# Holding the preparation of a second product behind the gate, the tanh and the h of each slot, in an attention and two-product chain on one core

## The chip, the cores and the metric

The kernel runs on one core of one Trainium2 chip. The metric is the device time in microseconds (us) of one execution. Five engines matter: TensorE (PE, with its weight loads as PEld), VectorE (DVE), ScalarE (ACT), GpSimd (POOL), and SyncE (SP), which here only issues transfers. Each has a queue of its own and works through it in order.

## The reference, cut to what matters

```python
def _attn_ref(q, k, v, p):               # q, k, v: 8 x 8 heads x 576 x 64, p: 8 x 8 x 32 x 64
    ...
    p_packed = sm_attn(p, k, v)
    out = sm_attn(q, p_packed, p_packed)
    return out.astype(np.float32)

def _moe_ref(x, w_in, w_out):            # x: 4608 x 512, w_in: 512 x 2048, w_out: 2048 x 512
    h = x @ w_in
    g = h * (1.0 / (1.0 + np.exp(-h)))
    return (g @ w_out).astype(np.float32)

def _moe2_ref(x, w1, w2, w3, w_out):     # w1, w2: 512 x 1024, w3: 1024 x 1024, w_out: 1024 x 512
    a = x @ w1
    b = x @ w2
    h = a * b @ w3
    return (h @ w_out).astype(np.float32)
```

The attention's output is the x of `_moe_ref`, and its output the x of `_moe2_ref`.

## The kernel before, in words

Every matrix product is in fp32r: a matrix is split into a high part (a rounded copy, `split_hi`, line 82 on ACT or 86 on DVE) and a low part (the difference, `split_lo`, line 91, on DVE or POOL), and `mm3` (lines 98 to 100) issues three matmuls for one: high by high, low by high, high by low.

**The slots.** The attention and the first product (`_moe_ref`) run in one loop over 256 items, called slots here and counted from 0. An item is a batch b (8), a half f of its 576 columns (288) and one of 16 blocks m of the hidden dimension. `emit_h` (from line 819) issues the 6 matmuls of h into one of two PSUM banks (`ps_h`); `emit_g` (from 831) issues tanh on ACT (`sg`, line 833), the gate on DVE (`gg`, line 838, which frees the bank) and the parts of `gg` (`gh` on ACT, `gl` on POOL); `emit_x2` (from 845) issues the 12 matmuls of the second half of the product (`ps_x`) three slots later (LAG = 3). When a half is through, ACT and DVE empty the four banks of `ps_x` (`xs`). `fetch` loads the weights of h slot by slot (`mr`, on SP's queue) several slots ahead of their use; DVE makes the high part (`mq`, line 86), POOL the low one.

**What rides beside it.** In each slot the loop calls generators, paced by `due`, that issue other work: the attention of the next batches, then, from slot 209 to slot 250, `prepare_second`. This prepares the weights of the second product. The weights of `_moe2_ref` arrive as 64-bit words (`raw`, loaded by SP at line 956) and are decoded: two ACT instructions (`ps_dec` and `raw`), two on DVE (`z`, line 176, and `raw`, line 178), one on POOL (`z`, line 182). Some were decoded earlier and come from DRAM (`z` from `late_d`). The generator has these pieces:

- `step()` takes one matrix. A block of `wo2` (8 of them, the first 8 steps) is split into `o`; a block of w3 is kept; two blocks of w1 or w2 together start `combine`, which puts 11 small steps on a list: sums and differences on DVE (`sums`, line 933), and parts `w12s` (high on ACT, low on DVE) that ACT's queue stores to DRAM.
- `some(2)` runs two entries of that list.
- `turn(n)` splits a block of w3 (`w3T`: high on ACT, low on DVE).
- `product(n)` multiplies a block of w3 by four blocks of `wo2` on PE (12 matmuls of 512 columns into `ps_w`); after every second one the sum is split (`w34s`) and stored by SP.

First come 11 calls with one `step()` each, then 18 rounds of two calls: a round has one product (from the third on), one turn (up to the 16th), and in each of its two calls a step, when one is due, and `some(2)`.

**What sets the order.** The instructions are not issued in the order of the program. A scheduler orders each engine's queue at build time by a simulation of its own, keeping dependencies; an instruction that is ready early by that simulation may be put far ahead of its place in the program. `tc.issue_after(x)` binds the instructions inside the block, on the engine of x alone, to places behind x in that queue. It adds an order, no semaphore. The dictionary `behind` holds the latest such x; before the change it has the latest tanh as `behind["sg"]` and the latest gate as `behind["gg"]`, and `fetch` and the decoding of earlier slots use them already.

After the loop follow the second product's own items, with PE busy nearly throughout.

Of the kernel before, what the change touches and what calls it, by code (L numbers as in the profile page):

```python
# [23 lines left out]
def attention_swiglu_chain(  # L24
# [35 lines left out]
    KM2 = DF2 // 128  # L60
# [18 lines left out]
    V, A, T, G, DMA = nc.vector, nc.scalar, nc.tensor, nc.gpsimd, nc.sync  # L79
# [4 lines left out]
    def split_hi(hi, src, on_vector=False):  # L84
        if on_vector:
            V.tensor_copy(out=hi, in_=src)  # L86
        else:
            act_copy(hi, src)

    def split_lo(lo, src, hi, eng=None):  # L90
        (eng or V).tensor_tensor(out=lo, in0=src, in1=hi.bitcast(F32), op=ALU.subtract)  # L91

    def split(hi, lo, src, on_vector=False, eng=None):
        split_hi(hi, src, on_vector)
        split_lo(lo, src, hi, eng)

    def mm3(dst, wh, wl, xh, xl, start, stop):
        T.matmul(out=dst, lhsT=wh, rhs=xh, start=start, stop=False)  # L98
        T.matmul(out=dst, lhsT=wl, rhs=xh, start=False, stop=False)  # L99
        T.matmul(out=dst, lhsT=wh, rhs=xl, start=False, stop=stop)  # L100

    behind = {}

    def move(out, in_, eng=DMA):

        out, in_ = (x.bitcast(F32) if x.dtype == F32R else x for x in (out, in_))
        with tc.issue_after(behind[eng]) if eng in behind else ExitStack():
            return eng.dma_start(out=out, in_=in_)  # L108
# [3 lines left out]
    def store(out, in_, age=1):  # L112

        stores.append([age, out, in_])

    def flush():
        for x in list(stores):
            if x[0] <= 0:
                move(x[1], x[2], A)
                stores.remove(x)  # L120
            else:
                x[0] -= 1
# [33 lines left out]
    def bank(name):  # L156
        return ps_f.tile([128, 512], F32, tag="f", name=name)
# [94 lines left out]
    class Lane:  # L252
# [31 lines left out]
        def mm(self, dst, w, x, start, stop):  # L284

            if self.plain:
                T.matmul(out=dst, lhsT=w[0], rhs=x[0], start=start, stop=stop)
            else:
                mm3(dst, *w, *x, start, stop)
# [300 lines left out]
    def chain(units):  # L590

        seen = set()

        def once(i, what):
            if i < len(units) and (i, what) not in seen:
                seen.add((i, what))
                getattr(units[i], what)()

        i = 0
        while i < len(units):  # L600
            u = units[i]
            for what in ("load", "prepare", "turn0", "turn1", "load_v", "split_v0"):
                once(i, what)
            if i:
                units[i - 1].tail()
            once(i + 1, "load")
            for n, _ in enumerate(u.steps()):
                for what in u.HOOKS.get(n, []):
                    once(i + 1, what)
                yield  # L610
            i += 1
        units[-1].tail()
# [120 lines left out]
    start = chain(units)  # L733
# [85 lines left out]
    def emit_h(i):  # L819
        b, f, m = items[i]  # L820
        ps = ps_h.tile([128, HS], F32, tag="h", name="ps_h")
        w = slots[:, holds.index((b, m))]
        for x in range(2):
            mm3(
                ps, w[:, x, 0], w[:, x, 1],
                a2[b][:, x, 0, f * HS:(f + 1) * HS], a2[b][:, x, 1, f * HS:(f + 1) * HS],
                x == 0, x == 1,
            )
        return ps

    def emit_g(i, ps):
# [49 lines left out]
    late, late_srcs = [], []  # L881
# [45 lines left out]
    def left_factors(z, sums, part):  # L927

        a11, a21, a12, a22 = (z[y][:, 256 * i:256 * i + 256] for y in range(2) for i in range(2))
        s1, s2, s3, s4 = (sums[:, i] for i in range(4))  # L930

        def add(dst, p, q, op=ALU.subtract):
            V.tensor_tensor(out=dst, in0=p, in1=q, op=op)

        return [
            lambda: part(0, a11), lambda: part(1, a12), lambda: add(s1, a21, a22, ALU.add),
            lambda: part(2, a22), lambda: add(s2, s1, a11), lambda: part(3, s1),
            lambda: add(s3, a11, a21), lambda: part(4, s2), lambda: add(s4, a12, s2),
            lambda: part(5, s3), lambda: part(6, s4),
        ]  # L940

    def prepare_second():

        attn.close()
        with tc.tile_pool(name="dec2", bufs=1, side="right") as dp:
            zs = []
            ps_dec, ps_w = bank("ps_dec"), bank("ps_w34")

            def load():
                n = len(zs) + KM2  # L950
                if n < MID:
                    zs.append(dp.tile([128, 512], F32, tag="z", name="z", bufs=6))
                    move(out=zs[-1], in_=late_d[n])
                else:
                    zs.append(dp.tile([128, 512], U64, tag="raw", name="raw", bufs=3))
                    DMA.dma_start(out=zs[-1], in_=late_srcs[n])

            o = [dp.tile([128, 2, 512], F32R, name=f"wo2_{j}") for j in range(KM2)]
            z3, z12 = {}, {}
            later = []  # L960

            def combine(n):
                z = [z12.pop(2 * n + y) for y in range(2)]
                sums = dp.tile([128, 4, 256], F32, tag="sums", name="sums", bufs=2)
                x, kt = divmod(n, 2)

                def part(j, src):
                    t = dp.tile([128, 2, 2, 128], F32R, tag="w12s", name="w12s", bufs=4)
                    split(t[:, :, 0], t[:, :, 1], src.rearrange("p (j n) -> p j n", j=2))
                    store(out=w12_d[:, :, x, kt, j], in_=t, age=0)  # L970

                later.extend(left_factors(z, sums, part))

            def some(n):
                for _ in range(min(n, len(later))):
                    later.pop(0)()

            used = [0]

            def step():  # L980
                n = used[0]
                used[0] += 1
                while len(zs) < min(n + 3, len(late) - KM2):
                    load()
                (kind, i), z = late[n + KM2], zs[n]
                if n + KM2 >= MID:
                    z = Decode(z, dp.tile([128, 512], I32, tag="z", name="z", bufs=6), ps_dec).z
                if kind == "o":
                    split(o[i][:, 0], o[i][:, 1], z, on_vector=True)
                elif kind == "3":  # L990
                    z3[i] = z
                else:
                    z12[i] = z
                    if i % 2:
                        combine(i // 2)

            w3T = {}

            def turn(n):
                t = dp.tile([128, 2, 4, 128], F32R, tag="w3T", name="w3T", bufs=3)  # L1000
                split(t[:, 0], t[:, 1], z3.pop(n).rearrange("p (j n) -> p j n", j=4))
                w3T[n] = t

            def product(n):
                i, f = divmod(n, 2)
                t = w3T.pop(n)
                for j in range(4):
                    w = o[4 * f + j]
                    mm3(ps_w, t[:, 0, j], t[:, 1, j], w[:, 0], w[:, 1], f == 0 and j == 0, f == 1 and j == 3)
                if f == 1:  # L1010
                    t = dp.tile([128, 2, 512], F32R, tag="w34s", name="w34s")
                    split(t[:, 0], t[:, 1], ps_w)
                    move(out=w34_d[i], in_=t)

            for n in range(KM2 + 3):
                step()
                yield
            for n in range(2 * KM2 + 2):
                if n > 1:
                    product(n - 2)  # L1020
                if n < 2 * KM2:
                    turn(n)
                for y in range(2):
                    if used[0] < min(len(late) - KM2, KM2 + 3 + 3 * (n + y) // 2):
                        step()
                    some(2)
                    yield
            some(len(later))
            flush()
            flush()  # L1030
# [3 lines left out]
    ins = []  # L1034
# [14 lines left out]
    for b in range(2, B - 2, 2):  # L1049
        n, at0 = b + 2, b * H2  # L1050
# [108 lines left out]
    def all_steps():  # L1159
        yield from start  # L1160
        yield from prepare_second()
# [228 lines left out]
```

## Time and profile before

| | |
|---|---|
| median of 3 runs | 1453.51 us (1453.17 to 1454.55) |
| the profiled execution, its own time | 1451.29 us |
| its span | 1449.5 us |
| mean granted TensorE clock | 0.991 |
| busy: PE, PEld | 1397.1 us (96%), 1310.8 us (90%) |
| busy: DVE | 908.6 us (63%) |
| busy: ACT | 672.1 us (46%) |
| busy: POOL | 598.6 us (41%) |

The profile is of one execution; the span runs from its first to its last instruction. Busy time is the time in which an engine has an instruction at work; an engine that waits for a semaphore isn't busy. The granted clock is a share of TensorE's full speed of 2.4 GHz; its other level is 1.2 GHz, so a mean between 0.5 and 1 says how much of a stretch was spent at which. The wait of an engine is put down to the instruction that released it. Lines are those of the kernel before.

### The profile page before, as it was taken

How to read it: one execution, taken by the hardware profiler on the slowest of the kernel's cores; microseconds unless marked ns; L12 is line 12 of the kernel's file. 1: busy time of each engine (PE TensorE's matmuls, PEld its weight loads, DVE VectorE, ACT ScalarE, POOL GpSimd, SP SyncE). 2: the span in 40 equal slices, each digit the busy share in tenths (PEclk: the TensorE clock that was granted, in tenths of full speed). 3: DMA queues.
4: the chain of work that ended last, by engine and by line, in shares of the span. 5: the costliest groups of instructions: out<-in, count | busy, mean ns of one | idle time of the engine just before them, and what ended most of it. 6: DMA issues, size and time to landing. Idle time of an engine off the chain costs nothing.

```text
span 1449.5 us, 25884 instructions
## 1 busy us (share of the span) xinstructions
PE 1397.1 (96%) x9548; PEld 1310.8 (90%) x9548; DVE 908.6 (63%) x1695; ACT 672.1 (46%) x1466; POOL 598.6 (41%) x626
## 2 busy tenths in 40 slices
PE   7799899999999999999989999999999999999998
PEld 5488799899999999999878998899999999999998
DVE  5897866569775588667897435745364454545453
ACT  6866555565665556654465433422132232323221
POOL 3778755856879657686476333300000000000000
PEclk9999999999999999999999999999999999999999
DMA  8597545845567444562686339011010101101000
GB/s 317 192 311 247 170 140 168 264 139 151 161 205 226 142 134 141 168 181 86 231 267 203 108 133 355 9 59 30 30 59 1 59 12 48 48 12 59 1 30 30
DMA packets 135967, 193.07 MB, mean 133 GB/s; under 512 B 14496, under 2 KB 92576, under 8 KB 135328
## 3 DMA queue, kind: packets, MB, share of 16 engines
q1 hardware_dynamic: 125344, 178.82, 38.4%
q10 hardware_dynamic: 10496, 12.59, 2.5%
q8 instruction: 75, 1.23, 0.3%
q14 instruction: 52, 0.43, 0.1%
HBM read 132.38 MB, written 58.98 MB: 132 GB/s over the span
## 4 chain that ended last, share of the span: by engine, by line
PE 68%; DVE 12%; DMA 7%; ACT 5%; issue 4%; POOL 2%; SPq 2%; ACTq 0%; DVEq 0%; POOLq 0%
PE ps_ab L1225 24%; PE ps_x L100 5%; PE ps_x L98 5%; PE ps_x L99 5%; PE ps_o L98 5%; PE ps_o L99 5%; PE ps_o L100 5%; PE ps_h L98 3%; PE ps_h L100 3%; PE ps_h L99 3%; DVE gg L838 1%; SPq L108 1%; DMA z<-late_d 1%; DVE sbd L244 1%; DVE mq L86 1%
## 5 line engine op out<-in xcount | busy, mean ns | idle before, releaser
L98 PE MATMUL ps_x<-gh,wo 128*128 128x288 f32 x1024 | 303.2, 300 | 6.2 <-DVE xs L875 2.0
L99 PE MATMUL ps_x<-gh,wo 128*128 128x288 f32 x1024 | 301.3, 297 | 0.0
L100 PE MATMUL ps_x<-gl,wo 128*128 128x288 f32 x1024 | 285.9, 298 | 2.3 <-POOL gl L91 2.2
L91 POOL TENSOR_TENSOR gl<-gg,gh 128x288 fp32r<-128x288 f32 x256 | 227.5, 892 | 110.9 <-ACT gh L82 94.9
L1225 PE MATMUL ps_ab<-xct,w 128*128 128x256 f32 x1728 | 222.3, 283 | 1.4 <-DVE r L1246 1.4
L1225 PEld LDWEIGHTS ps_ab<-xct,w 128*128 128x128 f32 x1728 | 214.9, 190 | 2.6 <-DVE r L1246 1.6
L98 PEld LDWEIGHTS ps_x<-gh,wo 128*128 128x128 f32 x1024 | 194.3, 190 | 11.4 <-DVE xs L875 3.6
L82 ACT ACTIVATE gh<-gg 128x288 fp32r<-128x288 f32 x256 | 112.7, 443 | 183.1 <-DVE gg L838 174.5
L99 PEld LDWEIGHTS ps_x<-gh,wo 128*128 128x128 f32 x1024 | 194.4, 190 | 2.2 <-issue 1.2
L100 PEld LDWEIGHTS ps_x<-gl,wo 128*128 128x128 f32 x1024 | 187.7, 190 | 5.5 <-POOL gl L91 4.3
L91 POOL TENSOR_TENSOR mq<-mr,mq 128x256 fp32r<-128x256 f32 x168 | 131.2, 781 | 113.7 <-DVE mq L86 47.1
L1225 PE MATMUL ps_ab<-xcb,w 128*128 128x256 f32 x1296 | 177.2, 283 | 0.0
L98 PE MATMUL ps_h<-a,mq 128*128 128x288 f32 x512 | 156.5, 306 | 21.4 <-DVE gg L838 17.2
L838 DVE SCALAR_TENSOR_TENSOR gg<-sg,ps_h 128x288 f32<-128x288 f32 x256 | 114.5, 447 | 96.1 <-ACT sg L833 48.8
L1225 PEld LDWEIGHTS ps_ab<-xcb,w 128*128 128x128 f32 x1296 | 168.1, 189 | 4.3
L1246 DVE TENSOR_TENSOR r<-p,ps_ab 128x512 f32<-128x512 f32 x72 | 49.2, 683 | 182.9 <-PE ps_ab L1225 182.7
L99 PE MATMUL ps_h<-a,mq 128*128 128x288 f32 x512 | 152.4, 298 | 0.0
L100 PE MATMUL ps_h<-a,mq 128*128 128x288 f32 x512 | 152.0, 297 | 0.1
L833 ACT ACTIVATE sg<-ps_h 128x288 f32<-128x288 f32 x256 | 102.7, 404 | 62.1 <-PE ps_h L100 44.1
L98 PEld LDWEIGHTS ps_h<-a,mq 128*128 128x128 f32 x512 | 96.8, 189 | 30.9 <-DVE gg L838 24.0
L82 ACT ACTIVATE p<-ps_ab 128x512 f32<-128x512 f32 x72 | 43.1, 598 | 145.5 <-PE ps_ab L1225 139.1
L99 PE MATMUL ps_o<-w,abl 128*128 128x512 f32 x280 | 110.0, 393 | 0.0
(173 smaller groups left out, 2649.2 us busy)
## 6 DMA issues: line engine op xcount, KB each, us to landing
mr<-m_d SPq DMA_DIRECT2D x144, 128.0 KB, 2.6
raw<-in_moe_w_dram SPq DMA_DIRECT2D x32, 512.0 KB, 4.4
wz<-wi_d SPq DMA_DIRECT2D x48, 256.0 KB, 3.7
m_d<-ms SPq DMA_DIRECT2D x96, 128.0 KB, 3.0
x_d<-xs SPq DMA_DIRECT2D x20, 576.0 KB, 3.6
raw<-in_moe_w_out_dram SPq DMA_DIRECT2D x22, 512.0 KB, 4.2
out_dram<-ob SPq DMA_DIRECT2D x36, 256.0 KB, 2.0
vr<-in_v_dram SPq DMA_DIRECT2D x14, 640.0 KB, 4.1
```

The costliest lines, as they stand in the source:

```text
L82: A.activation(out=dst, in_=src, func=ACTF.Copy, scale=mul)
L86: V.tensor_copy(out=hi, in_=src)
L91: (eng or V).tensor_tensor(out=lo, in0=src, in1=hi.bitcast(F32), op=ALU.subtract)
L98: T.matmul(out=dst, lhsT=wh, rhs=xh, start=start, stop=False)
L99: T.matmul(out=dst, lhsT=wl, rhs=xh, start=False, stop=False)
L100: T.matmul(out=dst, lhsT=wh, rhs=xl, start=False, stop=stop)
L108: return eng.dma_start(out=out, in_=in_)
L244: (act_copy if plain else V.tensor_copy)(dst[r, 0, :, r], src[r])
L833: ins = A.activation(out=sg, in_=ps, func=ACTF.Tanh, scale=0.5)
L838: ins = V.scalar_tensor_tensor(out=gg, in0=sg, scalar=1.0, in1=ps, op0=ALU.add, op1=ALU.mult)
L1225: T.matmul(out=bank[:, x], lhsT=w[:, wp], rhs=xt[:, kt, xp], start=first and (x, kt, n) == (0, 0, 0), stop=last and (x, kt, n) == (1, 1, 2 ...
L1246: V.tensor_tensor(out=dst, in0=p, in1=q, op=op)
```

## The change

The change puts the parts of `prepare_second` inside blocks that hold their instructions behind instructions of the slot in which they are issued: on ACT behind the slot's tanh (`sg`), on DVE behind its gate (`gg`), and, for `product` and `turn`, on PE behind the last matmul of its h (`h`). Instructions on POOL and transfers on SP's queue get no such order. Besides, the high parts of the 8 blocks of `wo2` are made by ACT, no longer by DVE.

```diff
     def mm3(dst, wh, wl, xh, xl, start, stop):
         T.matmul(out=dst, lhsT=wh, rhs=xh, start=start, stop=False)
         T.matmul(out=dst, lhsT=wl, rhs=xh, start=False, stop=False)
-        T.matmul(out=dst, lhsT=wh, rhs=xl, start=False, stop=stop)
+        return T.matmul(out=dst, lhsT=wh, rhs=xl, start=False, stop=stop)
...
+    def hold(*names):
+
+        stack = ExitStack()
+        for x in names:
+            stack.enter_context(tc.issue_after(behind[x]))
+        return stack
...
         for x in range(2):
-            mm3(
+            ins = mm3(
                 ps, w[:, x, 0], w[:, x, 1],
                 a2[b][:, x, 0, f * HS:(f + 1) * HS], a2[b][:, x, 1, f * HS:(f + 1) * HS],
                 x == 0, x == 1,
             )
+        behind["h"] = ins.ins
         return ps
...
                 if kind == "o":
-                    split(o[i][:, 0], o[i][:, 1], z, on_vector=True)
+                    split(o[i][:, 0], o[i][:, 1], z)
...
             for n in range(KM2 + 3):
-                step()
+                with hold("sg", "gg"):
+                    step()
                 yield
             for n in range(2 * KM2 + 2):
-                if n > 1:
-                    product(n - 2)
-                if n < 2 * KM2:
-                    turn(n)
+                with hold("sg", "gg", "h"):
+                    if n > 1:
+                        product(n - 2)
+                    if n < 2 * KM2:
+                        turn(n)
                 for y in range(2):
-                    if used[0] < min(len(late) - KM2, KM2 + 3 + 3 * (n + y) // 2):
-                        step()
-                    some(2)
+                    with hold("sg", "gg"):
+                        if used[0] < min(len(late) - KM2, KM2 + 3 + 3 * (n + y) // 2):
+                            step()
+                        some(2)
                     yield
```

What the scheduler makes of it is read from the order of the queues, here at three places. (Line numbers behind the new function are higher by 7 or 8 in the changed kernel.)

DVE's queue before, from the gate of slot 210 on (`wo_7` is the last block of `wo2`, `w3T` and `w12s` low parts of w3 and of the combined w1 and w2):

```order
L838 SCALAR_TENSOR_TENSOR gg<-sg,ps_h 128x288
L86 CAST mq<-mr 128x2x128
L91 TENSOR_TENSOR wo_7_9885<-z,wo_7_9885 128x512
L933 TENSOR_TENSOR sums<-z 128x256 x2
L91 TENSOR_TENSOR w3T<-z,w3T 128x512
L91 TENSOR_TENSOR w12s<-z,w12s 128x2x128 x2
L176 TENSOR_SCALAR z<-ps_dec 128x512
L178 SCALAR_TENSOR_TENSOR raw<-ps_dec,raw 128x512
L91 TENSOR_TENSOR w12s<-z,w12s 128x2x128
L933 TENSOR_TENSOR sums<-sums,z 128x256
```

and in the changed kernel, from the gates of slots 205 to 209 on, which stand side by side:

```order
L846 SCALAR_TENSOR_TENSOR gg<-sg,ps_h 128x288 x5
L86 CAST mq<-mr 128x2x128
L91 TENSOR_TENSOR wo_0_9878<-z,wo_0_9878 128x512
L91 TENSOR_TENSOR wo_1_9879<-z,wo_1_9879 128x512
L846 SCALAR_TENSOR_TENSOR gg<-sg,ps_h 128x288
L86 CAST mq<-mr 128x2x128
L883 TENSOR_SCALAR xs<-ps_x_9395 128x288
L91 TENSOR_TENSOR wo_2_9880<-z,wo_2_9880 128x512
L883 TENSOR_SCALAR xs<-ps_x_9397 128x288
L846 SCALAR_TENSOR_TENSOR gg<-sg,ps_h 128x288
```

Where the last `wo2` block and the first combined parts stood in slot 210, the first blocks of `wo2` stand now; the rest has moved to later slots.

DVE's queue in the changed kernel, from the gate of slot 222 on, the first of four slots (222, 229, 236, 243) with up to 12 instructions:

```order
L846 SCALAR_TENSOR_TENSOR gg<-sg,ps_h 128x288
L86 CAST mq<-mr 128x2x128
L91 TENSOR_TENSOR w3T<-z,w3T 128x512
L941 TENSOR_TENSOR sums<-z 128x256
L941 TENSOR_TENSOR sums<-sums,z 128x256
L183 TENSOR_SCALAR z<-ps_dec 128x512
L185 SCALAR_TENSOR_TENSOR raw<-ps_dec,raw 128x512
L91 TENSOR_TENSOR w12s<-z,w12s 128x2x128 x2
L91 TENSOR_TENSOR w12s<-sums,w12s 128x2x128
L183 TENSOR_SCALAR z<-ps_dec 128x512
L185 SCALAR_TENSOR_TENSOR raw<-ps_dec,raw 128x512
```

These steps stood in slots 210 to 214 before.

ACT's queue before, from the tanhs of slots 217 and 218 on, which stand side by side:

```order
L833 ACTIVATE sg<-ps_h 128x288 x2
L82 ACTIVATE raw<-raw 128x512
L82 ACTIVATE w12s<-z 128x2x128 x2
L82 ACTIVATE ps_dec<-raw 128x512
L82 ACTIVATE gh<-gg 128x288 x2
L82 ACTIVATE w12s<-sums 128x2x128
L108 DMA w_d<-w12s 256x1x256 x2
```

and in the changed kernel, from the tanh of slot 222 on, up to the next tanh:

```order
L841 ACTIVATE sg<-ps_h 128x288
L82 ACTIVATE w3T<-z 128x512
L82 ACTIVATE raw<-raw 128x512 x2
L82 ACTIVATE ps_dec<-raw 128x512
L115 DMA w_d<-w12s 256x1x256
L82 ACTIVATE gh<-gg 128x288
L82 ACTIVATE w12s<-z 128x2x128 x2
L82 ACTIVATE w12s<-sums 128x2x128
L82 ACTIVATE ps_dec<-raw 128x512
L115 DMA w_d<-w12s 256x1x256 x3
```

The tanhs stood in pairs with preparation behind each pair; now each slot has its tanh, and the preparation of that slot stands between two of them, stores (`w_d`) included.

## Rows read from the trace of the kernel before

**Rows 1.** Busy time, share of the span and instructions of each engine (the page's part 1).
```profile
PE 1397.1 (96%) x9548; PEld 1310.8 (90%) x9548; DVE 908.6 (63%) x1695; ACT 672.1 (46%) x1466; POOL 598.6 (41%) x626
```

**Rows 2.** Stages: us, busy PE, PEld, DVE, ACT, POOL, then PEclk, DMA share, GB/s.
```profile
600.00:689.56 89.56, 89.56 (x647) 87.73 (x647) 58.75 (x108) 50.41 (x113) 67.99 (x74) 1.00 0.53 155
700.00:720.00 20.00, 17.87 (x107) 16.39 (x106) 19.86 (x34) 12.09 (x29) 10.77 (x12) 0.91 0.73 249
720.00:740.00 20.00, 17.17 (x101) 15.32 (x100) 20.00 (x32) 12.83 (x28) 15.43 (x16) 0.91 0.75 234
...
760.00:780.00 20.00, 17.26 (x103) 15.51 (x102) 16.95 (x30) 13.23 (x31) 13.92 (x15) 0.91 0.76 256
...
800.00:820.00 20.00, 20.00 (x127) 18.55 (x126) 12.39 (x23) 9.88 (x22) 6.71 (x7) 1.00 0.37 132
```

**Rows 3.** Waits of PE from 700 to 790 us: total, times, longest.
```profile
PE ps_h L98 <- DVE gg L838: 5.1, 6, 1.8
PE ps_x L98 <- DVE xs L875: 1.4, 2, 1.0
```

**Rows 4.** Timeline of ACT at five slots: start, us, instruction [idle before <-releaser].
```profile
689.56 0.41 ACT L833 ACTIVATE sg<-ps_h 128x288 f32<-128x288 f32 x1 [0.73 <-PE ps_h L100]
...
843.77 0.41 ACT L833 ACTIVATE sg<-ps_h 128x288 f32<-128x288 f32 x1 [0.94 <-PE ps_h L100]
...
848.91 0.41 ACT L833 ACTIVATE sg<-ps_h 128x288 f32<-128x288 f32 x1 [3.69 <-PE ps_h L100]
...
856.43 0.41 ACT L833 ACTIVATE sg<-ps_h 128x288 f32<-128x288 f32 x1 [0.27 <-PE ps_h L100]
...
858.81 0.41 ACT L833 ACTIVATE sg<-ps_h 128x288 f32<-128x288 f32 x1 [0.95 <-PE ps_h L100]
```

**Rows 5.** Groups of DVE's instructions, 689 to 861 us: xcount, busy us, mean ns, idle before.
```profile
L838 DVE SCALAR_TENSOR_TENSOR gg<-sg,ps_h 128x288 f32<-128x288 f32 x46 | 20.5, 446 | 18.0 <-ACT sg L833 11.5 <-issue 4.5 <-POOL gl L91 2.0
L86 DVE CAST mq<-mr 128x256 fp32r<-128x256 f32 x32 | 17.6, 551 | 2.8 <-DMA mr<-m_d 2.8
L91 DVE TENSOR_TENSOR w12s<-sums,w12s 128x256 fp32r<-128x256 f32 x16 | 14.1, 907 | 0.0
L91 DVE TENSOR_TENSOR w3T<-z,w3T 128x512 fp32r<-128x512 f32 x16 | 14.1, 885 | 8.0 <-ACT w3T L82 8.0
L176 DVE TENSOR_SCALAR z<-ps_dec 128x512 int32<-128x512 int32 x20 | 13.6, 680 | 0.3 <-ACT ps_dec L82 0.2
L178 DVE SCALAR_TENSOR_TENSOR raw<-ps_dec,raw 128x512 int32<-128x512 int32 x20 | 13.5, 677 | 0.0
L91 DVE TENSOR_TENSOR w12s<-z,w12s 128x256 fp32r<-128x256 f32 x12 | 7.2, 616 | 0.8 <-ACT w12s L82 0.8
...
L933 DVE TENSOR_TENSOR sums<-z 128x256 f32<-128x256 f32 x8 | 6.5, 821 | 3.0 <-POOL z L182 3.0
...
L86 DVE CAST wo<-z 128x512 fp32r<-128x512 f32 x8 | 4.3, 543 | 3.2 <-DMA z<-late_d 3.2
```

**Rows 6.** ACT by tile and line: ns shortest/median/longest of `wo` and of the stores; group of `raw`.
```profile
L82 ACT ACTIVATE wo<-z x16: 613/629/639, 49.4 to 155.7; 128x512 fp32r<-128x512 f32 x16
...
L108 ACTq DMA_DIRECT2D w_d<-w12s x28: 520/521/893, 711.8 to 812.4; - x28
...
L82 ACT ACTIVATE raw<-raw 128x512 int32<-128x512 uint32 x20 | 13.6, 678 | 9.6 <-DMA raw<-in_moe_w_dram 5.8 <-DVE z L176 2.0 <-POOL gl L91 1.8
```

**Rows 7.** DVE: lengths of `w12s` (shortest/median/longest ns), and two instructions in the timeline.
```profile
L91 DVE TENSOR_TENSOR w12s<-sums,w12s x16: 411/878/1535, 717.4 to 811.7; 128x256 fp32r<-128x256 f32 x16
...
759.30 0.68 DVE L176 TENSOR_SCALAR z<-ps_dec 128x512 int32<-128x512 int32 x1
759.90 0.68 DVE L178 SCALAR_TENSOR_TENSOR raw<-ps_dec,raw 128x512 int32<-128x512 int32 x1
```

**Rows 8.** Waits of DVE from 705 to 780 us, the longest.
```profile
DVE sums L933 <- POOL z L182: 2.2, 1, 2.2
```

**Rows 9.** Waits of PE from 860 to 930 us, the longest.
```profile
PE ps_o L98 <- ACT abh L82: 2.0, 1, 2.0
```

## Prediction

> **What bounds the kernel now.** The page comes first: TensorE (PE) is busy for 96% of the span, VectorE (DVE) for 63%, and ScalarE (ACT) and GpSimd (POOL) for less than half [rows 1]. By this average nothing done to DVE could pay. So the next view is the table by stages, which is where the average breaks. From 600 to 689 us PE is busy all the time at full clock beside a DVE that is busy for two thirds. From 700 to 780 us it is the other way round: DVE is busy for 99 to 100% of the first slices (85% of the last), PE loses two to three of every 20 us, and its mean granted clock falls to 0.91. At 800 us PE is whole again [rows 2]. The waits of PE in that stretch name the queue: `ps_h` waits for `gg` on DVE, `ps_x` waits for `xs`, which stands in the same DVE queue and in ACT's [rows 3].
>
> What the stretch costs is read from the starts of `sg` (the tanh, one for each slot). The ends are slot 205 at 689.56 and slot 250 at 858.81, 169.25 us apart. A slot that PE runs undisturbed takes 858.81 - 856.43 = 2.38 us; one with a 12-matmul product of the preparation takes 848.91 - 843.77 = 5.14 us, so the product is 2.76 [rows 4]. 45 slots and 16 products should take 45 x 2.38 + 16 x 2.76 = 151.3 us. **18.0 us are lost**, and no change in the order of this preparation can win more. A part of them is clock: a slice of 20 us at a mean of 0.91 spent 18% of its time, 3.6 us, at the lower of the two levels, 1.2 GHz in place of 2.4, where half the work is done: 1.8 us for each of the three slices that read 0.91 [rows 2]. These falls follow waits of PE and should go with them.
>
> **The change, part by part.** No instruction waits for anything new: `hold` fixes only the place in the queue of each engine. Work and number of instructions stay, but for 8 casts.
>
> *The casts.* 8 high parts leave DVE, 8 x 0.543 = 4.3 us [rows 5], and come to ACT at the 0.63 us that the same cast of `wo` takes there [rows 6], 5 us. They stand in slots 209 to 215 behind a tanh and a `gh` (0.4 us each), so 1.5 us in a slot of 2.4: hidden on ACT. Were that cover gone, the price is those 5 us at most.
>
> *The slots of the first steps (209 to 220).* DVE's queue held, before, the work of much later slots here. Counted in the order and priced by [rows 5] (low parts of `wo2`, `w34s` like `z`; `xs` like `gg`): 83 instructions, 56 us. One DVE instruction starts 0.08 us before the end of the one in front (`z` at 759.30 lasts 0.68, `raw` starts at 759.90 [rows 7]), so 83 x 0.08 = 6.6 come off: 49 us. PE had 12 x 2.38 = 28.6 us there and four to five products. Every later `gg` stood behind that debt. With the change the same slots hold 36 instructions, 17 us. The debt isn't made.
>
> *The dense slots (221 to 246).* The work comes here instead. Slots 221 to 233 hold 83 DVE instructions: 13 `gg`, 12 `mq`, 24 `z` and `raw`, 7 `w3T`, 6 and 8 `w12s`, 8 `sums`, 3 `w34s`, 2 `xs`, 55.4 us by [rows 5], less 6.6 is **48.8 us**; PE needs 13 x 2.38 + 7 x 2.76 = **50.3 us**. Slots 234 to 246: 47.3 - 5.6 = 41.7 against 53.0. So DVE is now just faster than PE where it was far slower. The worst slots (222, 229, 236, 243 alike) hold up to 12 instructions: 0.446 + 0.551 + 0.885 + 2 x 0.821 + 2 x 0.680 + 2 x 0.677 + 2 x 0.616 + 0.907 = 8.4, less 1.0 is 7.4 us. The next `gg` is queued behind them, and the h two slots on needs its bank. From the end of `gg` 222 to the start of h 225 PE has 5.14 + 5.14 + 2.38 - 2.0 = 10.7 us of its own work (2.0: the six h are 6/18 of 2.38, 0.8; `sg` 0.41 [rows 4], `gg` 0.45 [rows 5], and 0.3 for the hand-overs). So 3 us are spare for what DVE waits within the slot, and what is left over runs on into the next slots, where only 1.5 us more come free by 233.
>
> *Waits inside the held slots.* The trace of before cannot show these. The lower bound is the saturated stretch, where DVE, free to take other work, waited over 1 us only once, 2.2 us in 75 [rows 8]; in 48 us that is 1.5, inside the spare. The upper bound: ACT does its share of a worst slot strictly between DVE's instructions. That share there is 2 decodes (0.68 + 0.63), a `w3T` and 3 `w12s` (0.63 at most) and 4 stores, each of which holds ACT's queue for 0.52 us: 7.2 us [rows 6]. If half of it is exposed, 3.6 us in each of four slots are 14.4; less 6 that are spare in the two dense stretches, some 8 us of stall, and two falls of the clock at 1.8: 12. I take 3 us, near the lower end, because the order of each queue is already one in which a high part stands several instructions ahead of its low part.
>
> *The moved transfers.* The 20 `raw` loads and 8 `w34s` stores on SP and the 28 `w12s` stores on ACT's queue go later, out of slices with a DMA share of 0.73 to 0.76 into slices of 0.37 [rows 2], so they collide less. The `mr` loads stand on SP behind `raw` loads, which wait for POOL's `z` three decodes back; DVE's cast `mq` waited 2.8 us for one in the whole stage [rows 5], and I cost that at nothing, since the slot weights are fetched several slots ahead; if that cover goes it is one such wait, 2.8 us.
>
> *What follows.* The last `w12s` now stands in slot 246 and the last `w34s` where it was, before slot 250, whose end starts the loads of the second product. Four slots, two with a product, are 15 us for the last stores to land. The seam behind the stage, where PE waits 2.0 us for `abh` [rows 9], is later work in the same order and moves along with the rest.
>
> *Sum.* 18.0 lost, 3 kept: **15 us gained**. The profiled execution took 1451.3 us (span 1449.5), so 1436.3; its place is 2.2 us below the median of the three runs, 1453.5. Against that median: **1438.5 us**.
>
> **A rule to weigh.** DVE's instructions with two inputs in SBUF differ widely in length: the low part `w12s` from `sums` took 0.411 at least, 0.878 in the median, 1.535 at most [rows 7]. My sum takes the means, since POOL ran beside DVE for 0.54 to 0.77 of those slices [rows 2] and its work isn't changed.
> The Trainium skill, page "SBUF — State Buffer", section "Who interferes with whom", says that a VectorE instruction with two SBUF inputs and a GpSimd instruction that reads SBUF exclude each other on a shared pair of ports, the later one blocking fully. It speaks against packing decodes and low parts into the same slots: were every such instruction blocked, the dense slots would go by the longest durations, as rival 2 works out. The spread above agrees that something of this kind is at work.
>
> **Rivals.**
> 1. *The chain through ACT, DVE and POOL is tight, and half of the cure goes.* For it: the upper bound above. Against it: [rows 8]. Stall 8 to 13, gain 5 to 10: about 1446.
> 2. *The two-input instructions of the dense slots mostly meet a POOL instruction, and DVE stays the bound.* From the mean [rows 5] to the longest, 1.535 [rows 7], is 0.63 for 16 `w12s` from `sums`, 0.92 for 12 from `z`, 0.65 for 16 `w3T` and 0.71 for 16 `sums`: 43 us in all if every one does. Spare between 221 and 246 is 103.3 - 90.5 + 3 = 16 us. At three quarters of the 43, 32 us, the stall is 16: 1451.5, no change. Against it: the mean was reached in a stretch where POOL ran beside DVE just as much.
> 3. *ACT's queue becomes the bound.* The place is the three `w12s` stores at the end of a worst slot, in front of the next tanh: they wait for DVE's low parts, the tanh behind them gives the next `gg`, and DVE waits for that. Preparation on ACT in slots 221 to 246 (20 decodes, 28 `w12s`, 21 `w3T` and `w34s`, 28 stores) is at most 72 us by [rows 6]. It decides for slower once nearly half of it, 34 us, is not beside DVE's work, since 90.5 + 34 is the 103 of PE, 3 of spare and the 18 of before. At 44 us the stage loses 28: 10 more than now, 1463. Against it: ACT's shares are issued slots ahead, and DVE was the engine others waited for.
>
> That the change doesn't do what it says is no rival: the orders of DVE and ACT show every step behind its slot.
>
> **How the numbers follow.** The forecast has 0.62, with a range of its own of 1434.8 (all 18.0 and 0.7 of scatter) to 1443; rival 1 has 0.22, rival 2 0.08, rival 3 0.08. The range takes in the forecast and most of rival 1: 1434.5 to 1447.5, leaving out 0.2. This kernel's runs tell 0.2%, 2.9 us, from no change. Faster: the forecast, rival 1 and a share of rival 2, 0.87. Within 0.2%: 0.06 from rival 2 and the ends of the others. Slower: 0.07, nearly all rival 3.
>
> **What would show it.** If right: between `sg` 205 and `sg` 250 some 154 us instead of 169; no slice there with DVE at 99%; PE's wait for `gg` under 2 us; no granted clock under 1.00; `sg` on ACT and `gg` on DVE no longer in pairs. Rival 1 shows as waits of `ps_h` for `gg` or `ps_w` for `w34s` at 225, 232 and 239; rival 2 as means of `w12s` and `w3T` over 1.2 us; rival 3 as `gg` waiting for `sg` while ACT waits for `w12s` low parts. The prediction is wrong if the loss is in another place than slots 205 to 250, the seam behind them above all.

## The result, and the profile after

The changed kernel takes **1438.13 us** (median of 4 runs, 1436.07 to 1439.83) against 1453.34 us for the kernel before on the same chip (1450.78 to 1454.55). The ratio is 0.9897, with a 95% interval of 0.9878 to 0.9916: faster by 1.0%, 15.2 us. Forecast were 1438.5 us and 15 us.

The page's first part, busy time by engine, answers to [rows 1]. The number of PE's and POOL's instructions is the same, the span is shorter by 13.4 us:

```profile
span 1436.1 us, 25890 instructions
...
PE 1390.7 (97%) x9548; PEld 1308.4 (91%) x9548; DVE 901.6 (63%) x1687; ACT 672.2 (47%) x1474; POOL 605.5 (42%) x626
```

DVE has 8 instructions fewer and ACT 8 more: the casts. The share of DVE is 63% as before, so the average shows nothing of what happened. The stages do (columns as in [rows 2]: us, busy PE, PEld, DVE, ACT, POOL, then granted clock, DMA share, GB/s):

```profile
700.00:720.00 20.00, 20.00 (x153) 20.00 (x152) 13.17 (x28) 11.45 (x28) 15.24 (x16) 1.00 0.58 186
720.00:740.00 20.00, 20.00 (x135) 19.00 (x135) 14.26 (x25) 10.92 (x26) 13.28 (x14) 1.00 0.35 97
740.00:760.00 20.00, 19.55 (x130) 18.32 (x129) 18.63 (x32) 13.87 (x34) 15.15 (x16) 1.00 0.81 268
760.00:780.00 20.00, 18.52 (x114) 16.80 (x113) 18.40 (x30) 10.58 (x25) 13.23 (x13) 1.00 0.77 255
780.00:800.00 20.00, 20.00 (x127) 18.50 (x127) 17.07 (x28) 12.27 (x27) 12.61 (x11) 1.00 0.73 237
800.00:820.00 20.00, 20.00 (x126) 18.47 (x126) 17.56 (x29) 14.72 (x34) 12.56 (x12) 1.00 0.63 219
```

From 700 to 740 us, where DVE was full and PE short of work, DVE is now busy for two thirds and PE all the time. The work that left is back from 740 to 820 us, where DVE is busy for 85 to 93% and PE loses 1.9 us in all (0.45 from 740 to 760, 1.48 from 760 to 780). The granted clock is 1.00 in every slice. The waits of PE from 690 to 845 us answer to [rows 3]; a single line is left:

```profile
PE ps_w L98 <- DVE w34s L91: 1.9, 2, 1.5
```

PE no longer waits for a gate. What is left is the product, which needs the bank of `w34s`. The tanhs of slots 205 and 250 in the timeline of ACT answer to [rows 4]:

```profile
690.22 0.41 ACT L841 ACTIVATE sg<-ps_h 128x288 f32<-128x288 f32 x1 [0.73 <-PE ps_h L100]
...
844.05 0.41 ACT L841 ACTIVATE sg<-ps_h 128x288 f32<-128x288 f32 x1 [0.58 <-PE ps_h L100]
```

The stage takes 844.05 - 690.22 = 153.8 us instead of 169.25; 151.3 would be without loss, so 2.5 of the 18.0 us are left. That is 15.4 us gained here. The profiled executions differ by less, 13.4 us, because this one came 0.7 us later to slot 205 (work that the change doesn't touch) and needed 592.05 us from slot 250 to its end, against 590.7.

How a worst slot runs is seen in DVE's timeline from the gate of slot 222 to the next:

```profile
731.59 0.44 DVE L846 SCALAR_TENSOR_TENSOR gg<-sg,ps_h 128x288 f32<-128x288 f32 x1
731.96 1.05 DVE L86 CAST mq<-mr 128x256 fp32r<-128x256 f32 x1
...
736.57 1.85 DVE L91 TENSOR_TENSOR w12s<-z,w12s 128x256 fp32r<-128x256 f32 x2
738.34 0.41 DVE L91 TENSOR_TENSOR w12s<-sums,w12s 128x256 fp32r<-128x256 f32 x1
738.68 0.68 DVE L183 TENSOR_SCALAR z<-ps_dec 128x512 int32<-128x512 int32 x1
739.28 0.68 DVE L185 SCALAR_TENSOR_TENSOR raw<-ps_dec,raw 128x512 int32<-128x512 int32 x1
740.14 0.45 DVE L846 SCALAR_TENSOR_TENSOR gg<-sg,ps_h 128x288 f32<-128x288 f32 x1 [0.18 <-ACT sg L841]
```

and in ACT's at the end of the same slot:

```profile
736.68 0.65 ACT L82 ACTIVATE ps_dec<-raw 128x512 f32<-128x512 f32 x1 [1.73 <-DVE raw L185]
737.01 2.64 ACTq L115 DMA_DIRECT2D w_d<-w12s  x3
739.69 0.41 ACT L841 ACTIVATE sg<-ps_h 128x288 f32<-128x288 f32 x1 [2.37 <-DMA w_d<-w12s]
```

DVE works without a gap until the next gate, 740.14 - 731.59 = 8.55 us later, and that gate waits 0.18 us for its tanh. The tanh itself stood 2.37 us behind the three stores, which waited for low parts of DVE: the loop of rival 3 is there, but DVE is busy meanwhile, so it costs the gate 0.2 us.

### The profile page after: what moved, and what is told of

It reads as the page before. It is cut to its first block, busy times and chain, and to the rows that moved or that the text cites. A ratio compares the mean times of both kernels' runs of the same rounds, so it can differ in the third digit from the quotient of the medians.

```text
span 1436.1 us, 25890 instructions
## 1 busy us (share of the span) xinstructions
PE 1390.7 (97%) x9548; PEld 1308.4 (91%) x9548; DVE 901.6 (63%) x1687; ACT 672.2 (47%) x1474; POOL 605.5 (42%) x626
## 4 chain that ended last, share of the span: by engine, by line
PE 70%; DVE 9%; DMA 7%; issue 4%; POOL 4%; ACT 4%; SPq 2%; ACTq 0%; DVEq 0%; POOLq 0%
PE ps_ab L1236 24%; PE ps_x L100 6%; PE ps_x L98 6%; PE ps_x L99 6%; PE ps_o L98 5%; PE ps_o L99 5%; PE ps_o L100 5%; PE ps_h L98 3%; PE ps_h L100 3%; PE ps_h L99 3%; SPq L115 2%; DMA mr<-m_d 1%; DMA m_d<-ms 1%; POOL z L189 1%; DVE sbd L251 1%
## 5 line engine op out<-in xcount | busy, mean ns | idle before, releaser
L100 PE MATMUL ps_x<-gl,wo 128*128 128x288 f32 x1024 | 289.1, 297 | 1.9 <-POOL gl L91 1.6
L91 POOL TENSOR_TENSOR mq<-mr,mq 128x256 fp32r<-128x256 f32 x168 | 136.7, 814 | 109.0 <-DVE mq L86 54.4
L100 PE MATMUL ps_o<-w,abh 128*128 128x512 f32 x280 | 109.5, 391 | 0.0
```

The source lines that it names most:

```text
L100: return T.matmul(out=dst, lhsT=wh, rhs=xl, start=False, stop=stop)
```

## Experiments

Each ratio is to the kernel before on the same chip. "Stage" is the time from the tanh of slot 205 to that of slot 250 in its profiled execution; 151.3 us would be without loss.

| kernel | hold on ACT (`sg`) | on DVE (`gg`) | on PE (`h`) | casts on | median us | ratio, 95% interval | stage us |
|---|---|---|---|---|---|---|---|
| before | - | - | - | DVE | 1452.4 to 1453.3 | 1 | 169.25 |
| the change | yes | yes | yes | ACT | 1438.13 | 0.9897, 0.9878 to 0.9916 | 153.8 |
| the change again | yes | yes | yes | ACT | 1437.12 | 0.9890, 0.9873 to 0.9908 | 153.8 |
| hold only | yes | yes | yes | DVE | 1436.81 | 0.9890, 0.9871 to 0.9909 | 153.8 |
| casts only | - | - | - | ACT | 1447.42 | 0.9964, 0.9949 to 0.9978 | 164.1 |
| h only | - | - | yes | ACT | 1447.68 | 0.9967, 0.9953 to 0.9981 | 163.4 |
| first steps only | first 11 | first 11 | - | ACT | 1450.48 | 0.9992, 0.9979 to 1.0004 | 167.9 |
| gate only | - | yes | - | ACT | 1447.59 | 0.9966, 0.9952 to 0.9981 | 163.8 |
| no gate | yes | - | yes | ACT | 1433.80 | 0.9873, 0.9853 to 0.9892 | 152.2 |
| no gate again | yes | - | yes | ACT | 1434.19 | 0.9872, 0.9851 to 0.9893 | 152.0 |
| tanh, casts on DVE | yes | - | - | DVE | 1435.88 | 0.9882, 0.9864 to 0.9899 | 153.8 |

My theory was that DVE's queue is what costs: work of later slots in front of the gates, a debt of DVE to PE. The debt by the order, used below, adds up DVE's work less PE's, slot by slot and never below zero, with the durations of [rows 5].

**The two halves of the change.** The hold without the casts:

```diff
-                    split(o[i][:, 0], o[i][:, 1], z)
+                    split(o[i][:, 0], o[i][:, 1], z, on_vector=True)
```

> Holds as in the change, casts of wo2 back on DVE. Theory (DVE's debt to PE is what costs): the 4.3 us of casts fall into slots 209 to 215, where DVE has 10 us to spare; the debt of DVE from slot 221 on is that of the change. 1438 to 1440 us, PE loses 2 to 4 us between the tanhs of slots 205 and 250. Rival (the casts are half of the gain, since they are taken off the engine that bounds): 1443 to 1446.

1436.81 us, a little under the 1438 to 1440 expected, and a stage of 153.8 us, the change's to a tenth. And the casts without any hold:

```diff
-                    split(o[i][:, 0], o[i][:, 1], z, on_vector=True)
+                    split(o[i][:, 0], o[i][:, 1], z)
```

> Casts on ACT as in the change, no hold. Theory: the order still puts later work into early slots; the largest debt of DVE to PE by counting the order goes from 10.9 us before to 7.9, so PE loses 10 to 15 us of the 18 between the tanhs of slots 205 and 250: 1446 to 1451 us. Rival (casts carry it): under 1442.

1447.42 us, stage 164.1, so 12.8 us are still lost. Both came as the theory had it. The halves don't add up: the casts are worth 5 us alone and nothing beside the hold, which is worth 15.6 alone.

**Products behind the h of their slot, alone.** Only `product` and `turn` stand in a block, `hold("h")`; casts on ACT.

> Hold only on PE (product behind the slot's h), casts on ACT, no hold on ACT and DVE. Theory: PE's order isn't the bound; DVE's debt by the order is 7.0 us: as with the casts alone, 1445 to 1451 us. Rival (products in front of the h of their slot delay the tanh, and that is what the change cures): under 1442.

1447.68 us, as with the casts alone. PE's order isn't what the change cures. In fact, once the hold behind the tanh is there, taking the one behind h away leaves every queue as it is, instruction for instruction, with the hold behind the gate or without it.

**The first 11 steps, alone.**

```diff
-                with hold("sg", "gg", "h"):
+                with hold():
...
-                    with hold("sg", "gg"):
+                    with hold():
```

(only in the 18 rounds)

> Hold only on the first 11 steps, none on the 18 rounds. Theory: the rounds' work still runs ahead (debt by the order up to 9.7 us): PE loses 10 to 16 us in the stage, 1446 to 1451 us. Rival (the debt is made by the steps of wo2 alone): under 1442.

1450.48 us, stage 167.9: no faster than before. (16.6 us are lost, a little over what was expected; the profiled execution was the slowest of ten, 1454.43 us.) Holding the steps of `wo2` doesn't take the debt away; the rounds' work that runs ahead of its slot makes it.

**Which queue must be held.** Without the hold behind the gate:

```diff
-                with hold("sg", "gg", "h"):
+                with hold("sg", "h"):
...
-                with hold("sg", "gg"):
+                with hold("sg"):
```

> Hold behind the tanh on ACT and behind h on PE, not behind the gate on DVE. Theory: almost every step on DVE needs a high part or a decode of ACT, so the hold on ACT alone already keeps DVE's work in its slot (debt by the order 3.9 us against 3.5 in the change): 1437 to 1441 us. Rival (the hold on DVE's own queue is the part that acts): 1446 or more.

1433.8 us: better than expected, and better than the change. As the hold behind h changes no queue, this kernel orders ACT's queue alone. And the other way round, the gate alone (`hold("gg")` in all three places):

> Hold only behind the gate on DVE, none on ACT and PE. Theory (either hold alone keeps DVE's debt small, 2.3 us by the order): within 2 us of the change, stage 152 to 156 us. Rival (ACT's preparation, which may then run ahead of the tanhs, delays tanh and with it the gate): 3 to 8 us slower than the change, with gates waiting for tanhs.

1447.59 us, stage 163.8. **Here the theory fell.** By the order DVE owes PE at most 2.3 us, no more than in the change. DVE even has its work in the same slots: from 205 to 250 each slot holds the DVE instructions that it holds in the change, but for one `xs` that moved by a slot. Between the gates of slots 209, 221, 234 and 247 that makes 36, 83 and 70 (83, 54 and 44 in the kernel before). Still 12.5 us are lost, and the 5.3 us gained are no more than the casts bring alone. Nor is DVE full, as the stages of this kernel show (columns as above):

```profile
770.00:790.00 20.00, 17.59 (x107) 15.77 (x106) 16.99 (x28) 11.73 (x26) 11.75 (x12) 1.00 0.71 235
790.00:810.00 20.00, 17.75 (x115) 16.29 (x113) 15.20 (x23) 11.11 (x25) 10.24 (x9) 1.00 0.59 202
810.00:830.00 20.00, 18.89 (x103) 16.94 (x104) 14.64 (x25) 12.00 (x27) 10.52 (x11) 0.91 0.46 160
```

From 770 to 810 us PE loses over two of every 20 us, from 810 to 830 over one, beside a DVE that is busy for 73 to 85%. What DVE waited for from 731 to 790 us, and PE from 690 to 860 us:

```profile
DVE gg L846 <- ACT sg L841: 5.2, 3, 2.4
DVE w34s L91 <- ACT w34s L82: 2.5, 2, 1.3
```

```profile
PE ps_w L98 <- DVE w34s L91: 4.5, 2, 2.4
PE ps_h L98 <- DVE gg L846: 2.6, 3, 1.4
```

Gates wait for tanhs; and on ACT from 731 to 790 us the two longest lines are these:

```profile
ACT ps_dec L82 <- DVE raw L185: 8.4, 7, 2.2
ACT raw L82 <- DMA raw<-in_moe_w_dram: 4.3, 4, 2.8
```

In the change, on the same chip, gates waited 0.4 us for tanhs in the like stretch (729 to 784 us):

```profile
DVE gg L846 <- ACT sg L841: 0.4, 2, 0.2
```

So ACT, left free, takes decodes of later slots in front of a tanh. The timelines of PE (end of the h), ACT and DVE show it, first at slot 229, then at slot 233:

```profile
762.39 0.29 PE L100 MATMUL ps_h<-a,mq 128*128 128x288 f32 x1
764.62 0.67 ACT L82 ACTIVATE raw<-raw 128x512 int32<-128x512 uint32 x1 [2.84 <-DMA raw<-in_moe_w_dram]
766.08 0.39 ACT L841 ACTIVATE sg<-ps_h 128x288 f32<-128x288 f32 x1
766.50 0.46 DVE L846 SCALAR_TENSOR_TENSOR gg<-sg,ps_h 128x288 f32<-128x288 f32 x1 [2.39 <-ACT sg L841]
...
783.08 0.29 PE L100 MATMUL ps_h<-a,mq 128*128 128x288 f32 x1
786.87 0.64 ACT L82 ACTIVATE ps_dec<-raw 128x512 f32<-128x512 f32 x1 [2.21 <-DVE raw L185]
788.34 0.40 ACT L841 ACTIVATE sg<-ps_h 128x288 f32<-128x288 f32 x1
788.77 0.46 DVE L846 SCALAR_TENSOR_TENSOR gg<-sg,ps_h 128x288 f32<-128x288 f32 x1 [1.60 <-ACT sg L841]
```

The tanh of slot 229 starts 3.4 us after its h is through, that of slot 233 5.0 us after. In front of the first stands a decode that waits for its load, in front of the second one that waits for its turn at the one bank `ps_dec`. That bank DVE must empty, and DVE, now held, does so only behind a gate that needs a tanh. The rival of that run had the right mechanism, though it put the price at 3 to 8 us and it was 10.5 (1447.59 against 1437.12 for the change on this chip): it is ACT's queue that has to be held.

**The least that does it.** Only `hold("sg")`, and the casts of `wo2` back on DVE, where nothing holds them:

> The least that should do it: hold behind the tanh on ACT alone, casts of wo2 on DVE as before, nothing on DVE's or PE's queue. Theory (the steps' high parts and decodes on ACT pace DVE by their data; the free casts are 4.3 us in slots with 10 us to spare): equal to the one without the hold behind the gate within 1.5 us, stage 151.5 to 154 us. Rival (free casts and low parts of wo2 on DVE start the debt again): 4 us slower or more.

1435.88 us, stage 153.8. One order, on ACT's queue, carries the whole gain. DVE's steps follow by their data, since their high parts and decodes come from ACT: its queue holds 31, 83 and 69 instructions between the gates named above. The kernel is 1.7 us behind the version without the gate on this chip (below), a little over the 1.5 expected. PE waited for gates here, from 701 to 705 us, where the free casts and low parts of `wo2` stand in front of gates; so the rival acts, but in small:

```profile
PE ps_h L98 <- DVE gg L846: 1.1, 2, 0.9
```

**Is the version without the gate better?** Both again, on one chip:

> The changed kernel once more, on the chip of the three others. Both theories: a ratio to the kernel before of 0.988 to 0.992, 153 to 155 us between the tanhs of slots 205 and 250.

> The kernel without the hold behind the gate once more. Theory (the hold behind the gate delays a few sums on DVE and with them the low part of w34s, for which PE's next product waits): 1 to 3 us faster than the change on the same chip, stage 151.5 to 153 us. Rival (its 1433.8 us was chance): equal to the change within 0.5 us.

1434.19 us (1433.53 to 1436.33) against 1437.12 us (1435.95 to 1438.67), and the stages are 152.0 and 153.8, each as in its first run. In the version's first run the waits of PE in the stage come down to

```profile
PE ps_w L98 <- DVE w34s L91: 0.6, 1, 0.6
```

from 1.9 us. By the order some `sums` stand in earlier slots there (they read nothing that ACT writes), and in front of the low part of `w34s` there is less. So 1.8 of the 2.9 us are explained; the other 1.1, outside the stage, are not, and may be scatter. **This version was ahead of the change both times**, in the ratio (0.9873 and 0.9872 against 0.9897 and 0.9890, with intervals that overlap) and in the stage, and it differs from the change by leaving one hold out.

**How near DVE is to being the bound.** One DVE instruction more, which nobody reads, at 11 places of the changed kernel:

```diff
+            def extra():
+                V.tensor_tensor(out=spare, in0=spare, in1=spare, op=ALU.add)
...
                         some(2)
+                        if y == 0 and 2 <= n < 13:
+                            extra()
```

> The change with 11 more DVE instructions (128 x 512, two inputs in SBUF, in place, nobody reads them) in the dense slots, one in each of rounds 2 to 12. Theory: DVE is nearly the bound there, 8 to 9 us more work on a spare of 1.5 us in slots 221 to 233 and 3 at the head: 2 to 6 us slower than the change, 1440 to 1444 us. Rival (DVE isn't near the bound, PE's loss before came from something else): within 1 us of the change.

and the same behind each of the first 11 steps instead:

> The change with the same 11 DVE instructions, one behind each of the first 11 steps (slots 209 to 219). Theory: 17 us of DVE work beside 28.6 of PE, so 9 us more are free: within 1 us of the change, 1437 to 1439.5 us. Rival (any DVE work in the stage costs): as the other one, 1440 to 1444.

1438.70 us (ratio 0.9907, 0.9892 to 0.9922) and 1439.13 us (0.9907, 0.9891 to 0.9924): neither can be told from the change by the median, so this pair misses as it was put (2 to 6 us were expected for the first, under 1 for the second). The stages are 156.4 and 155.1 us, 2.6 and 1.3 more than the change. DVE's busy time in the stage rose from 113.5 us to 120.4 and 124.6. So 7.0 us more of it cost 2.6 in the dense slots, and 11.1 us more cost 1.3 in the first ones: the direction fits the theory, though even the dense slots took in more than half.

**All generators held.** Every step that rides in a slot from 16 on, the attention's too, inside `hold("sg", "gg")`:

```diff
-                next(streams[y], None)
+                with hold("sg", "gg") if i >= KM else ExitStack():
+                    next(streams[y], None)
```

> The change, and every generator that rides in a slot from 16 on is held behind the slot's tanh and gate. Theory: the attention's DVE work, which can stand in front of a gate now (PE waits 6.3 us for gates between 155 and 690 us), stands behind it: 3 to 8 us faster than the change, 1430 to 1435 us. Rival (those gates are late for other reasons, and the attention's chains get longer): same or slower.

1446.37 us (0.9961, 0.9949 to 0.9972): 8 to 9 us slower than the change, a plain miss. The stage is nearly the change's, 154.3; the slots from 26 to 205 took 553.4 us, against 547.8 and 545.2 in the two runs of the change. PE's waits from 146 to 700 us there, and from 142 to 690 us in the change:

```profile
PE ps_h L98 <- DVE gg L846: 10.0, 11, 3.9
PE ps_s L98 <- DVE mbd L492: 6.5, 5, 2.2
```

```profile
PE ps_h L98 <- DVE gg L846: 8.4, 10, 2.7
PE ps_s L98 <- DVE mbd L492: 1.9, 4, 0.8
```

PE's own queue holds matmuls of the attention (`ps_s`) that need those steps (`mbd`) soon. Held behind the gates they come later, and PE waits for them with the next h behind.

## Why the prediction was right, and where its working was not

*The prize* was right: 18.0 us between the two tanhs, of which 15.4 came back. It came from two readings of the trace alone, an undisturbed slot with and without a product.

*What is kept* was put at 3 us between bounds of 0 and 12; it is 2.5. The waits inside the held slots, which the trace of before could not show, reached PE as 1.9 us. The worst slot was put at 7.4 us plus its waits; it took 8.55 with DVE working nearly all the time, so its instructions took longer than they were priced at, and its waits were next to nothing. The means of [rows 5] (0.885, 0.907 and 0.616 us for the three lines below) held in the sum, but not one by one:

```profile
L91 DVE TENSOR_TENSOR w3T<-z,w3T 128x512 fp32r<-128x512 f32 x16 | 13.9, 866 | 0.1
L91 DVE TENSOR_TENSOR w12s<-sums,w12s 128x256 fp32r<-128x256 f32 x16 | 12.1, 757 | 0.0
L91 DVE TENSOR_TENSOR w12s<-z,w12s 128x256 fp32r<-128x256 f32 x12 | 10.4, 894 | 0.0
```

That the forecast came within 0.4 us of the median is in part luck: the 3 us were picked between wide bounds, the sum of the dense slots (below) was short by 2.4, and the four runs themselves lie 3.8 us apart.

*The casts* were costed at nothing on ACT, which is right, and the run with the hold alone shows that they are worth nothing on DVE either once the hold is there.

*The mechanism failed in one step.* "Every later `gg` stood behind that debt. [...] The debt isn't made" put the whole cure on DVE's queue. The debt is real: a DVE at 99% fell to 66 to 71% over the two slices from 700 to 740 us, and in the kernel before, the whole list of DVE's waits from 709 to 785 us has no gate in it:

```profile
DVE sums L933 <- POOL z L182: 2.2, 1, 2.2
DVE w12s L91 <- ACT w12s L82: 0.8, 1, 0.8
DVE z L176 <- ACT ps_dec L82: 0.2, 1, 0.2
```

But not making the debt isn't enough. The kernel that holds DVE alone has DVE's work in the slots of the change, and keeps only a third of the gain, which the casts bring without it. The kernels that order ACT alone keep all of it. So it is ACT's preparation that had to be put behind the tanhs: left free, it feeds DVE's debt, and with DVE held it stands in front of the tanhs instead. I had counted ACT as the engine with time to spare (46% of the span) and priced its queue only as a danger of the change.

*"So DVE is now just faster than PE"* in the dense slots was too hopeful. Slots 221 to 233 were summed to 48.8 us of DVE beside 50.3 of PE. Between the gates of slots 221 and 234 the same 83 instructions kept DVE busy for 51.2 us (columns as in [rows 2]):

```profile
728.84:783.45 54.61, 52.69 (x331) 48.55 (x330) 51.21 (x83) 33.42 (x77) 37.60 (x37) 1.00 0.73 235
```

DVE is a little slower than PE there, and PE's 1.9 us of waits lie in this stretch.

*The rivals.* Rival 1's place was right, the product's wait for `w34s`, its size not (1.9 us instead of 8 to 13). Rival 2: no mean of a two-input instruction came near 1.2 us; the longest is 0.894. Rival 3: its loop stands in the timeline, at 0.2 us.

*The clock*: the three falls are gone, as forecast. Behind the stage the seam stayed: from 880 to 910 us the mean granted clock is 0.89, as it was in the like 30 us before. That it only moved along was right within 1.4 us.

## What to carry to other kernels

These runs are of one kernel; what follows is advice, not shown elsewhere. Where a scheduler may fill an engine's queue with work for later, look at the engine that feeds the others' chain, not only at the one that is full: an order on that queue alone (here ACT, behind each tanh) paces the rest by their data. Hold what nobody needs soon; held steps that another engine awaits soon cost more than they free, as the attention's steps did here. And price such a change by the undisturbed slot: what a stage loses against its own good slots is the most that any order can win.

## What the runs showed of the hardware

The same DVE instruction, 128 x 512 with both inputs in SBUF, took 0.68 us at least in either place, but twice that in the median among the decodes. Its lines by tile in the two loaded kernels (shortest/median/longest ns, first and last start), dense slots first:

```profile
L971 DVE TENSOR_TENSOR spare<-spare x11: 677/1441/1653, 731.7 to 807.3; 128x512 f32<-128x512 f32 x11
```

```profile
L971 DVE TENSOR_TENSOR spare<-spare x11: 679/927/1298, 701.7 to 724.5; 128x512 f32<-128x512 f32 x11
```

In the dense slots each of the seven that took 1.43 us or more overlaps in time the add with which POOL ends a decode (`z`, line 189); of the four short ones (0.68 to 0.72 us) three overlap none. That agrees with the Trainium skill, page "SBUF — State Buffer", section "Who interferes with whom", by which a VectorE instruction with two SBUF inputs contends with a GpSimd instruction that reads SBUF. No run here took GpSimd's work away to show it. The 11 took 13.1 us in the dense slots, but DVE's busy time grew by only 7.0, in part because its other instructions took 4.6 us less than in the change.

Losses of the same kind need not cost clock: the kernel with the casts alone lost 12.8 us in the stage at a mean granted clock of 1.00 (columns as in [rows 2]), where the kernel before, with 18.0, had three stretches at the lower level.

```profile
689.80:853.90 164.10, 155.86 (x1004) 143.61 (x1003) 110.01 (x199) 87.96 (x197) 89.70 (x98) 1.00 0.57 188
```
